# q for two tiles at a time behind k of the second one, G of both behind the next k

## The chip, the cores and the metric

The kernel runs on one core of one Trainium2 chip. The metric is device time in microseconds (us) of one execution, median of three runs. The core has five engines that work side by side, each in the order of its own program: TensorE (PE, with its weight loads as PEld), VectorE (DVE), ScalarE (ACT), GpSimd (POOL) and SyncE (SP), which here only issues DMAs and waits.

## The reference

Two blocks read x (2048 tokens of 640 numbers, bf16) and are added to it. The first is linear attention with 32 heads of 20 on the normalized xn, the second sends the 8 tokens with the largest router value through a gated MLP.

```python
xn = _layernorm(x)
# attention
q, k, v = split(xn @ wqkv)                    # 32 heads of 20
phi = lambda t: where(t > 0, t + 1, exp(t)) + 1e-6
pq, pk = phi(q), phi(k)
kv = einsum("bhsd,bhse->bhde", pk, v)
z = einsum("bhsd->bhd", pk)
num = einsum("bhqd,bhde->bhqe", pq, kv)
den = einsum("bhqd,bhd->bhq", pq, z)[..., None] + 1e-6
A = (num / den) @ wo
# eight tokens through the MLP
r = xn @ w_r
idx = argsort(-r)[:, :8]
y = (silu(xn[idx] @ w_gate) * (xn[idx] @ w_up)) @ w_down * sigmoid(r[idx])
B = xn + scatter(y, idx)
out = x + A + B
```

## The kernel before

The tokens are cut into 16 tiles of 128. v is never formed: instead of kv = pk' (xn wv) the kernel sums G = xn' pk over the tiles and multiplies by wv once. phi is written as min(exp(t), 1) + relu(t), so ACT makes two passes over the psum of k or q (Exp, Relu) and VectorE one that joins them.

The program is written out by hand: each engine executes its instructions in the order in which the source names them, and so do the DMA queues of SP, ACT and POOL. An instruction that waits holds up all behind it on its engine.

For each tile t there are these steps, by their names in the code:

- `ln_stats` (two `ln_half`, L163, and `ln_aggr`, L167) has VectorE take mean and variance of x; from tile 4 on POOL makes the reciprocal deviation out of it in four small steps (L171, L176, L178, L179).
- `ln_norm` (L191, VectorE) writes xn; from tile 3 on the same function issues a DMA transpose on SP (L196) that writes the tile's columns of xnT. Tiles 0 to 2 are transposed by TensorE (`tr_tile`) and copied out by `tr_evict`.
- `k_mm` (L236) makes k and, in a 641st column, the router value: five steps over D with 512 and 129 columns each, into the psum pair A. `k_phi` has ACT make both passes and copy the router value to r_all; `phi_vec` (L225, VectorE) writes pk.
- `q_mm` (L248) makes q transposed: 25 matmuls with wq as weights and 128 columns of xnT moving, into the psum pair B, then the two passes of ACT and one of VectorE (`q_phi`, L225) into pqT.
- `ga_mm` (L259) adds the tile's part of three fifths of G, three matmuls of 512 columns, with xn as weights and pk moving; its sums stay in the psum pair C and the bank D0 through the loop.

The loop over t issues, on TensorE, k(t), G(t-1), q(t). In the same round VectorE takes statistics of tile t + 3 and the norm of tile t + 2 (one more of each in round `CATCH` = 5, after which both are a tile further ahead), q of tile t - 1, and k of tile t. In the last rounds it also adds xn to x (`residual`, L360), and SP copies these sums to DRAM four tiles at a time (`keep`, L363).

`late_loads(t)` stands at the end of a round and issues the remaining loads on SP (L343), after the transposes that the round's norms issued: x of tiles 8 to 11 in round 2, x of tiles 12 to 15 in round 5, then wg and wu in rounds 6 to 11, wv and wo in 12 to 15, wd after the loop. `small_consts(t)` gives POOL a few small constants in rounds 3 to 6 and VectorE three small steps in round 12.

Behind the loop: four transposes of the router values (`pr`), G of the last tile, sums of pk over the tokens (`zp`, whose four parts go through small DMAs on SP and ACT, L477), the other two fifths of G (`gb1` 32 matmuls of 512 columns, L489, and `gb2` 80 of 128, L590), among them the search for the eight tokens on VectorE, the denominators (`pden`, L571, which reads all of pqT) and the MLP's products (`gu`, for which POOL gathers eight columns of xnT, L537). Then kv, M = kv wo, and the output tile by tile (L743, L751), 16 x 10 matmuls.

Of the kernel before, what the change touches and what calls it, by code (L numbers as in the profile page):

```python
# [8 lines left out]
P = 128  # L9
# [22 lines left out]
CATCH = 5  # L32
# [12 lines left out]
def kernel(  # L45
# [173 lines left out]
    def phi_vec(dst, er, as3):  # L219
        e, r = er  # L220
        ea, ra = e[:], r[:]
        if as3:
            ea = ea.rearrange("p (k f) -> p k f", k=KC)
            ra = ra.rearrange("p (k f) -> p k f", k=KC)
        nc.vector.scalar_tensor_tensor(  # L225
            out=dst, in0=ea, scalar=1.0, in1=ra, op0=ALU.min, op1=ALU.add
        )
# [16 lines left out]
    def q_mm(t, tag="B"):  # L244
        ps = pair(tag, f"q{t}")
        for m in range(KC):
            for kc in range(KC):
                nc.tensor.matmul(  # L248
                    ps[:, m * P : (m + 1) * P],
                    lhsT=wq[:, kc, m::KC],  # L250
                    rhs=xnT[:, kc, t * P : (t + 1) * P],
                    start=(kc == 0 and m in (0, 4)), stop=(kc == KC - 1),
                    skip_group_check=True,
                )
        return ps

# [84 lines left out]
    def late_loads(t):  # L341
        def part(dst, src, a, b):
# [7 lines left out]
            12: (wv, wv_v, 0, 2), 13: (wv, wv_v, 2, KC), 14: (wo, wo_v, 0, 4), 15: (wo, wo_v, 4, 8),  # L350
            16: (wd, kcD, 0, 6), 17: (wd, kcD, 6, 12),
# [14 lines left out]
    qer = None  # L366

    def q_phi(t, er):
        phi_vec(pqT[:, :, t * P : (t + 1) * P], er, True)

    def k_phi(t, kp):
        ker = phi_act(kp, "k")
# [3 lines left out]

    kp = k_mm(0, "A")
    tr1a, tr1b = bank("D1", "tr1a").bitcast(BF16), pair("C", "tr1b").bitcast(BF16)
# [4 lines left out]
    ln_stats(3)  # L383
    ker = k_phi(0, kp)
    kp = k_mm(1, "B")
    qp = q_mm(0, "A")
    ln_norm(2)
    phi_vec(pk[:, 0, :], ker, False)
    tr2 = bank("D1", "tr2").bitcast(BF16)
    tr_tile(2, tr2, 0, KC)  # L390
    ker = k_phi(1, kp)
    eq0 = phi_act(qp, "q", lambda: tr_evict(2, tr2, 0, KC, nc.scalar.copy))
    ln_norm(3)
    ln_stats(4)
    ga_mm(0)
    phi_vec(pk[:, 1, :], ker, False)
    qp = q_mm(1, "B")
    q_phi(0, eq0)
    qer = phi_act(qp, "q")

    for t in range(2, T):
        kp = k_mm(t)
        ga_mm(t - 1)
        qp = q_mm(t)
        for u in (t + 3, t + 4) if t == CATCH else (t + 3 + (t > CATCH),):
            if u < T:
                ln_stats(u)
# [399 lines left out]
```

## Time and profile before

| | us |
|---|---|
| median of three runs (111.18 to 112.16) | 111.19 |
| the profiled execution | 111.62 |
| its span, first to last instruction | 109.9 |
| TensorE busy | 105.5 |
| VectorE busy | 86.1 |
| ScalarE busy | 55.1 |
| GpSimd busy | 37.9 |

The median is what the change is compared by. All durations that follow come from the one profiled execution; it is 0.43 us above the median, and 1.7 us of it lie outside the span. A row of the chain shows start, duration, engine, tile name, line and count; a row of a group shows line, engine, operation, output and inputs, form and count, then busy time, the mean duration in ns, and the idle time of the engine just before, with what ended it. The mean duration of a matmul counts its whole way through the array; what a matmul costs in a stream is the time from one start to the next.

### The profile page before, as it was taken

How to read it: one execution, taken by the hardware profiler on the slowest of the kernel's cores; microseconds unless marked ns; L12 is line 12 of the kernel's file. 1: busy time of each engine (PE TensorE's matmuls, PEld its weight loads, DVE VectorE, ACT ScalarE, POOL GpSimd, SP SyncE). 2: the span in 40 equal slices, each digit the busy share in tenths (PEclk: the TensorE clock that was granted, in tenths of full speed). 3: DMA queues.
4: the chain of work that ended last, by engine and by line, in shares of the span. 5: the costliest groups of instructions: out<-in, count | busy, mean ns of one | idle time of the engine just before them, and what ended most of it. 6: DMA issues, size and time to landing. Idle time of an engine off the chain costs nothing.

```text
span 109.9 us, 2999 instructions
## 1 busy us (share of the span) xinstructions
PE 105.5 (96%) x1183; PEld 69.3 (63%) x1183; DVE 86.1 (78%) x205; ACT 55.1 (50%) x102; POOL 37.9 (34%) x83
## 2 busy tenths in 40 slices
PE   6998999999999999999999999999999999999990
PEld 2456866777577766777667744447995555555560
DVE  6889999887999889875999896951348967698680
ACT  4037987778867797777977745068028000000000
POOL 5414195989889955770000000240008100000000
DMA  2998164930569999998859970899541289997333
GB/s 72 335 375 292 33 36 75 283 66 3 118 177 321 220 267 280 316 305 224 290 187 285 292 257 5 232 378 372 175 145 51 15 228 323 340 387 277 128 119 119
DMA packets 25358, 23.09 MB, mean 210 GB/s; under 512 B 10624, under 2 KB 24064, under 8 KB 25344
## 3 DMA queue, kind: packets, MB, share of 16 engines
q1 hardware_dynamic: 22784, 20.43, 66.5%
q10 hardware_dynamic: 2384, 2.43, 6.4%
q8 instruction: 9, 0.15, 0.6%
q0 software_dynamic: 176, 0.04, 0.6%
q14 instruction: 5, 0.04, 0.1%
HBM read 14.94 MB, written 5.81 MB: 189 GB/s over the span
## 4 chain that ended last, share of the span: by engine, by line
PE 76%; DVE 10%; POOL 8%; issue 3%; DVEq 0%; POOLq 0%
PE o L743 14%; PE k L236 13%; PE q L248 13%; PE gbA L489 6%; PE gaC L259 5%; PE warm L271 4%; PE gbC L590 4%; POOL sq L176 3%; DVE st L163 2%; PE gaD L259 2%; DVE pk L225 2%; PE M L728 2%; POOL sc L178 2%; DVE xn L191 2%; PE gu L606 2%
## 5 line engine op out<-in xcount | busy, mean ns | idle before, releaser
L248 PEld LDWEIGHTS <-wq 128*128 128x128 bf16 x400 | 24.2, 117 | 3.4
L236 PE MATMUL k<-wk,xnT 128*128 128x512 bf16 (+1 forms) x160 | 24.8, 301 | 0.3 <-ACT xnT L206 0.3
L248 PE MATMUL q<-xnT,wq 128*128 128x128 bf16 x400 | 24.9, 220 | 0.0
L743 PEld LDWEIGHTS <-pqT 128*128 128x128 bf16 x165 | 12.8, 98 | 9.3
L236 PEld LDWEIGHTS <-xnT 128*128 128x128 bf16 x160 | 12.3, 98 | 8.5 <-ACT xnT L206 0.9
L213 ACT ACTIVATE eq<-q 128x640 bf16<-128x640 f32 x16 | 11.2, 703 | 10.5 <-PE q L248 10.5
L225 DVE SCALAR_TENSOR_TENSOR pk<-ek,rk 128x640 bf16<-128x640 bf16 x16 | 13.2, 824 | 3.6 <-ACT rk L216 3.4
L743 PE MATMUL o<-M,pqT 128*128 128x512 bf16 x110 | 15.8, 300 | 0.0
L176 POOL TENSOR_TENSOR sq<-sq,half 128x1 bf16<-128x1 bf16 x16 | 12.5, 778 | 6.2 <-DVE sc L175 4.0
L163 DVE BATCH_NORM_STATS2 st<-x_sb 128x6 f32<-128x320 bf16 x32 | 14.1, 480 | 0.4 <-DMA x_sb<-in_A_x_dram 0.4
L225 DVE SCALAR_TENSOR_TENSOR pqT<-eq,rq 128x640 bf16<-128x640 bf16 x16 | 13.2, 823 | 0.7 <-ACT rq L216 0.7
L213 ACT ACTIVATE ek<-k 128x640 bf16<-128x640 f32 x16 | 11.3, 705 | 1.6 <-PE k L236 0.4
L751 DVE TENSOR_TENSOR o_t<-o,x_sb 128x640 bf16<-128x640 f32 x11 | 8.8, 820 | 3.3 <-DMA x_sb<-xcp 1.7
L216 ACT ACTIVATE rq<-q 128x640 bf16<-128x640 f32 x16 | 11.2, 700 | 0.0
L216 ACT ACTIVATE rk<-k 128x640 bf16<-128x640 f32 x16 | 11.2, 699 | 0.0
L259 PE MATMUL gaC<-pk,xn 128*128 128x512 bf16 x32 | 9.5, 378 | 0.2 <-DVE pk L225 0.2
L537 POOL COPY xsT<-xnT 128x5 bf16 x8 | 1.9, 312 | 21.7 <-DVE icol L551 21.7
L178 POOL TENSOR_TENSOR sc<-sq,neg 128x1 f32<-128x1 bf16 x12 | 8.6, 716 | 0.9
L191 DVE TENSOR_SCALAR xn<-x_sb,sc 128x640 bf16<-128x640 bf16 (+2 forms) x17 | 6.9, 412 | 1.2 <-POOL sc L179 1.0
L489 PE MATMUL gbA<-pk,xn 128*128 128x512 bf16 x32 | 7.3, 380 | 0.0
L360 DVE TENSOR_TENSOR x_sb<-x_sb,xn 128x640 bf16<-128x640 bf16 x16 | 7.0, 482 | 0.0
L259 PEld LDWEIGHTS <-xn 128*128 128x128 bf16 x48 | 4.0, 97 | 4.1 <-issue 0.4
(152 smaller groups left out, 120.4 us busy)
## 6 DMA issues: line engine op xcount, KB each, us to landing
xcp<-x_sb SPq DMA_DIRECT2D x4, 640.0 KB, 5.2
x_sb<-in_A_x_dram SPq DMA_DIRECT2D x3, 640.0 KB, 4.7
wd<-in_B_w_down_dram SPq DMA_DIRECT2D x2, 960.0 KB, 6.6
x_sb<-xcp SPq DMA_DIRECT2D x3, 640.0 KB, 6.8
wg<-in_B_w_gate_dram SPq DMA_DIRECT2D x2, 768.0 KB, 6.6
wu<-in_B_w_up_dram SPq DMA_DIRECT2D x2, 768.0 KB, 5.3
out_dram<-o_t ACTq DMA_DIRECT2D x8, 160.0 KB, 2.7
out_dram<-o_t SPq DMA_DIRECT2D x7, 160.0 KB, 3.4
```

Source lines behind the costliest of these rows:

```text
L163: nc.vector.bn_stats(out=stat[t][:, h, :], in_=x_sb[:, t, h * HW : (h + 1) * HW])
L176: nc.gpsimd.tensor_tensor(out=sq[:, 1:2], in0=sq[:, 0:1], in1=half[:], op=ALU.pow)
L178: nc.gpsimd.tensor_tensor(out=sc[:, 1:2], in0=sq[:, 1:2], in1=neg1[:], op=ALU.pow)
L191: nc.vector.tensor_scalar(out=xn[:, t, a:b], in0=x_sb[:, t, a:b], scalar1=sc[:, 0:1], scalar2=sc[:, 1:2], op0=ALU.subtract, op1=ALU.mult,)
L213: nc.scalar.activation(e[:], ps[:, 0:D], AF.Exp)
L216: nc.scalar.activation(r[:], ps[:, 0:D], AF.Relu)
L225: nc.vector.scalar_tensor_tensor(out=dst, in0=ea, scalar=1.0, in1=ra, op0=ALU.min, op1=ALU.add)
L236: nc.tensor.matmul(ps[:, a:b], lhsT=xnT[:, kc, t * P : (t + 1) * P], rhs=wk[:, kc, a:b], start=(kc == 0), stop=(kc == KC - 1),)
L248: nc.tensor.matmul(ps[:, m * P : (m + 1) * P], lhsT=wq[:, kc, m::KC], rhs=xnT[:, kc, t * P : (t + 1) * P], start=(kc == 0 and m in (0, 4)) ...
L259: nc.tensor.matmul(gaC[:, c * TBLK : (c + 1) * TBLK] if c < 2 else gaD[:], lhsT=xn[:, t, c * P : (c + 1) * P], rhs=pk[:, t, 0:TBLK], start ...
L489: nc.tensor.matmul(gbA[:, (c - 3) * TBLK : (c - 2) * TBLK], lhsT=xn[:, t, c * P : (c + 1) * P], rhs=pk[:, t, 0:TBLK], start=(t == 0), stop ...
L743: nc.tensor.matmul(ps, lhsT=pqT[:, m, t * P : (t + 1) * P], rhs=M[:, m, a:b], start=(m == 0), stop=(m == KC - 1),)
```

## The change

The loop becomes one over pairs of tiles (t, t + 1), t even. TensorE issues in each round: k(t+1), four fifths of q for both tiles (`q2_mm` with `LO`, 20 matmuls of 256 columns, pair B), k(t+2), the last fifth of q (`HI`, five matmuls, bank D1), G(t), G(t+1). ACT makes its passes over 1024 and 256 columns in place of 640, VectorE likewise (`q2_vec`), and joins q of pair t - 2 in the round of pair t. `CATCH` is 4: in rounds up to 4 statistics are four tiles past t at the head of the round and five at its end, from round 6 on five and six. Round 4 has the additional tile of statistics and norm. `small_consts` and `late_loads` of both tiles stand at the end of the round, and in the plan wd now comes before wv and wo. Ten of the residuals are added in rounds 10 to 14, two more among the steps of the token search, and the copies to DRAM follow them. The transposes of the router values stand between q of the last pair and its G. Behind the loop `pc` is issued after three tiles of `gb1` in place of four, the two tiles of `gb2` ahead of `gu` are placed behind it, `ph` follows eleven tiles in place of twelve, and q of the last pair is joined after the search.

```diff
 LN_FAST = 4
 WARM = 10
 LAST = (0, 320, 512, 640)
-CATCH = 5
+CATCH = 4
 
 BF16 = mybir.dt.bfloat16
 F32 = mybir.dt.float32
...
             )
         return ps
 
-    def q_mm(t, tag="B"):
-        ps = pair(tag, f"q{t}")
-        for m in range(KC):
+    def q2_mm(t, ps, ms):
+        for n, m in enumerate(ms):
             for kc in range(KC):
                 nc.tensor.matmul(
-                    ps[:, m * P : (m + 1) * P],
+                    ps[:, n * 2 * P : (n + 1) * 2 * P],
                     lhsT=wq[:, kc, m::KC],
-                    rhs=xnT[:, kc, t * P : (t + 1) * P],
-                    start=(kc == 0 and m in (0, 4)), stop=(kc == KC - 1),
+                    rhs=xnT[:, kc, t * P : (t + 2) * P],
+                    start=(kc == 0 and n % 2 == 0), stop=(kc == KC - 1),
                     skip_group_check=True,
                 )
         return ps
+
+    def q2_tile(tag):
+        return work.tile([P, KC, 2 * P], BF16, tag=tag, name=tag)
+
+    def q2_act(dst, func, ps, ms):
+        n = len(ms) * 2 * P
+        nc.scalar.activation(
+            dst[:, ms[0] : ms[-1] + 1, :].rearrange("p m f -> p (m f)"), ps[:, 0:n], func
+        )
+
+    def q2_vec(t, er, ms):
+        a, b = ms[0], ms[-1] + 1
+        nc.vector.scalar_tensor_tensor(
+            out=pqT[:, a:b, t * P : (t + 2) * P], in0=er[0][:, a:b, :], scalar=1.0,
+            in1=er[1][:, a:b, :], op0=ALU.min, op1=ALU.add,
+        )
+
+    LO, HI = (0, 1, 2, 3), (4,)
 
     def ga_mm(t):
         for c in range(3):
...
             2: (x_sb, x_v, 8, 12), 5: (x_sb, x_v, 12, 16),
             6: (wg, kcF, 0, 2), 7: (wg, kcF, 2, 4), 8: (wg, kcF, 4, 5),
             9: (wu, kcU, 0, 2), 10: (wu, kcU, 2, 4), 11: (wu, kcU, 4, 5),
-            12: (wv, wv_v, 0, 2), 13: (wv, wv_v, 2, KC), 14: (wo, wo_v, 0, 4), 15: (wo, wo_v, 4, 8),
-            16: (wd, kcD, 0, 6), 17: (wd, kcD, 6, 12),
+            12: (wd, kcD, 0, 6), 13: (wd, kcD, 6, 12), 14: (wv, wv_v, 0, 2), 15: (wv, wv_v, 2, KC),
+            16: (wo, wo_v, 0, 4), 17: (wo, wo_v, 4, 8),
         }
         if t in plan:
             part(*plan[t])
...
         nc.sync.dma_start(xcp_v[:, a:b, :], x_sb[:, a:b, :])
 
 
-    qer = None
-
-    def q_phi(t, er):
-        phi_vec(pqT[:, :, t * P : (t + 1) * P], er, True)
-
-    def k_phi(t, kp):
-        ker = phi_act(kp, "k")
+    def k_vec(t, er):
+        phi_vec(pk[:, t, :], er)
+
+    def k_phi(t, kp, between=None):
+        ker = phi_act(kp, "k", between)
         nc.scalar.copy(r_all[:, t : t + 1], kp[:, D : D + 1])
         return ker
 
-
+    ker = {}
     kp = k_mm(0, "A")
-    tr1a, tr1b = bank("D1", "tr1a").bitcast(BF16), pair("C", "tr1b").bitcast(BF16)
+    tr1a, tr1b = bank("D1", "tr1a").bitcast(BF16), pair("B", "tr1b").bitcast(BF16)
     tr_tile(1, tr1a, 0, 2)
     tr_evict(1, tr1a, 0, 2, nc.scalar.copy)
     tr_tile(1, tr1b, 2, KC)
     tr_evict(1, tr1b, 2, KC, nc.vector.tensor_copy)
-    ln_stats(3)
-    ker = k_phi(0, kp)
-    kp = k_mm(1, "B")
-    qp = q_mm(0, "A")
+    ln_half(3, 0)
     ln_norm(2)
-    phi_vec(pk[:, 0, :], ker, False)
-    tr2 = bank("D1", "tr2").bitcast(BF16)
+    ln_half(3, 1)
+    ln_aggr(3)
+    ker[0] = k_phi(0, kp)
+    kp = k_mm(1, "C")
+    tr2 = bank("D0", "tr2").bitcast(BF16)
     tr_tile(2, tr2, 0, KC)
-    ker = k_phi(1, kp)
-    eq0 = phi_act(qp, "q", lambda: tr_evict(2, tr2, 0, KC, nc.scalar.copy))
+    k_vec(0, ker[0])
     ln_norm(3)
-    ln_stats(4)
-    ga_mm(0)
-    phi_vec(pk[:, 1, :], ker, False)
-    qp = q_mm(1, "B")
-    q_phi(0, eq0)
-    qer = phi_act(qp, "q")
-
-    for t in range(2, T):
-        kp = k_mm(t)
-        ga_mm(t - 1)
-        qp = q_mm(t)
-        for u in (t + 3, t + 4) if t == CATCH else (t + 3 + (t > CATCH),):
-            if u < T:
-                ln_stats(u)
-        for u in (t + 2, t + 3) if t == CATCH else (t + 2 + (t > CATCH),):
-            if u < T:
-                ln_norm(u)
-        q_phi(t - 1, qer)
-        ker = k_phi(t, kp)
-        if t > 12:
-            residual(4 * (t - 13) + 3)
-        phi_vec(pk[:, t, :], ker, False)
-        qer = phi_act(qp, "q")
-        if 11 < t < T - 1:
-            for u in range(4 * (t - 12), 4 * (t - 12) + 3):
+    ker[1] = k_phi(1, kp, lambda: tr_evict(2, tr2, 0, KC, nc.scalar.copy))
+
+    eqp = None
+    for t in range(0, T, 2):
+        if t > 0:
+            kp = k_mm(t + 1)
+            k_vec(t, ker[t])
+            ahead = 4 + (t > CATCH)
+            if t + ahead < T:
+                ln_stats(t + ahead)
+            if t + ahead - 1 < T:
+                ln_norm(t + ahead - 1)
+            ker[t + 1] = k_phi(t + 1, kp)
+        lo = q2_mm(t, pair("B", f"qlo{t}"), LO)
+        if t > 0:
+            q2_vec(t - 2, eqp, LO)
+            q2_vec(t - 2, eqp, HI)
+        eqp = q2_tile("eq"), q2_tile("rq")
+        q2_act(eqp[0], AF.Exp, lo, LO)
+        if t == T - 2:
+            break
+        kp = k_mm(t + 2)
+        ker[t + 2] = k_phi(t + 2, kp)
+        q2_act(eqp[1], AF.Relu, lo, LO)
+        hi = q2_mm(t, bank("D1", f"qhi{t}"), HI)
+        q2_act(eqp[0], AF.Exp, hi, HI)
+        q2_act(eqp[1], AF.Relu, hi, HI)
+        if t == 0:
+            ln_stats(4)
+            k_vec(1, ker[1])
+            ln_stats(5)
+            ln_norm(4)
+        else:
+            if t == T - 4:
+                for u in range(2, 5):
+                    residual(u)
+            k_vec(t + 1, ker[t + 1])
+            if t == CATCH:
+                ln_stats(t + 5)
+            if t + ahead < T:
+                ln_norm(t + ahead)
+            if t == CATCH:
+                ln_stats(t + 6)
+                ln_norm(t + 5)
+            elif t + ahead + 1 < T:
+                ln_stats(t + ahead + 1)
+        if t == T - 6:
+            for u in range(2):
                 residual(u)
-        small_consts(t)
-        late_loads(t)
-        if t > 12:
-            keep(4 * (t - 13), 4 * (t - 12))
-
-
+        if t == T - 4:
+            for u in range(5, 8):
+                residual(u)
+            keep(0, 4)
+        ga_mm(t)
+        ga_mm(t + 1)
+        for u in (t, t + 1):
+            small_consts(u)
+            late_loads(u)
+
+
+    q2_act(eqp[1], AF.Relu, lo, LO)
+    for u in (8, 9):
+        residual(u)
+    keep(4, 8)
+    late_loads(T - 2)
+    late_loads(T - 1)
+    k_vec(T - 1, ker[T - 1])
     pr = bank("D1", "pr").bitcast(BF16)
...
+    ga_mm(T - 2)
+    ga_mm(T - 1)
+    hi = q2_mm(T - 2, bank("D1", "qhi"), HI)
+    q2_act(eqp[0], AF.Exp, hi, HI)
+    q2_act(eqp[1], AF.Relu, hi, HI)
...
     )
     spread(0, 1, cand[:, 0:1, :])
     spread(1, 2, split[:])
+    residual(10)
 
     zp = pair("A", "zp")
 
...
                 tile_position=(0, 32 * i),
             )
 
-    ga_mm(T - 1)
     for t in range(T):
         z_mm(t)
     GT = sb([P, KC, D], BF16, "GT", tag="wk")
...
                 start=(t == 0), stop=(t == T - 1),
             )
 
-    for t in range(4):
+    for t in range(3):
         gb1(t)
     pc = bank("D1", "pc")
     nc.tensor.matmul(
...
         pc[:, 32:64], lhsT=ones4[:], rhs=candm[:, 2].rearrange("p b c -> p (b c)"),
         start=False, stop=True,
     )
-    for t in range(4, T):
+    for t in range(3, T):
         gb1(t)
...
     nc.vector.tensor_reduce(out=idx8[:], in_=eq[:], op=ALU.add, axis=AX.X)
     idxi = sb([P, C], I32, "idxi")
     nc.vector.tensor_copy(idxi[:], idx8[:])
-    q_phi(T - 1, qer)
+    residual(11)
+    keep(8, 12)
+    q2_vec(T - 2, eqp, LO)
+    q2_vec(T - 2, eqp, HI)
     _, toks = nc.values_load_multi_w_load_instructions(
         idxi[0:1, :], engines=[ENG.Pool], min_val=0, max_val=S - 1,
         skip_runtime_bounds_check_because="positions found among the tokens",
...
                 start=(t == 0 and c in (0, 4)), stop=(t == T - 1),
                 skip_group_check=True,
             )
-
-    for t in range(2):
-        gb2(t)
 
 
     gu = pair("A", "gu")
...
             op=ALU.mult,
         )
 
-    for t in range(2, 12):
+    for t in range(11):
         gb2(t)
     ph = bank("D1", "ph").bitcast(BF16)
     for b in range(3):
...
         in0=ph[:, 0:FJ].rearrange("p (n c) -> p n c", c=32)[:, :, 0:C],
         in1=gtb[:].unsqueeze(1).to_broadcast([P, FC, C]), op=ALU.mult,
     )
-    for t in range(12, T):
+    for t in range(11, T):
         gb2(t)
     nc.scalar.copy(GT[:, :, TBLK:D], gbC[:, 0:D].rearrange("p (c f) -> p c f", c=KC))
 
```

14 lines of the change are left out of this document (5 added, 9 removed).

## The prediction, before the result was known

> **What bounds the kernel now.** I read the share of each engine first, then the stages, then the chain.
>
> ```profile
> PE 105.5 (96%) x1183; PEld 69.3 (63%) x1183; DVE 86.1 (78%) x205; ACT 55.1 (50%) x102; POOL 37.9 (34%) x83
> ...
> 14.00:28.00 14.00, 14.00 (x158) 10.12 (x155) 12.06 (x28) 10.75 (x21) 11.79 (x28) 1.00 0.43 87
> 28.00:48.00 20.00, 19.77 (x218) 14.13 (x216) 17.94 (x37) 15.65 (x30) 15.64 (x31) 1.00 1.03 255
> ```
>
> The columns of the stages are PE, weight loads, DVE, ACT and POOL. The last number is GB/s. TensorE is busy for all of 14 to 28 us and misses 0.23 us of 28 to 48 us: it is the bound, and VectorE is second, with 18 of 20 us. So only two things can move the time: fewer TensorE nanoseconds, or new gaps on TensorE. One tile of the loop in the chain:
>
> ```profile
> 33.02 0.43 PE gaC L259 x2
> 33.46 0.21 PE gaD L259
> 33.67 1.40 PE q L248 x25
> 35.07 1.38 PE k L236 x10
> ```
>
> That is 0.65 (G), 1.40 (q) and 1.38 (k): 3.43 us a tile, without a gap.
>
> **q for two tiles.** 50 matmuls with 128 columns become 25 with 256. One with 128 costs 1.40 / 25 = 56 ns, one with 512 costs 0.43 / 2 = 215 ns; between them a matmul costs 2.9 ns and 0.414 ns a column, so one with 256 costs 109 ns. A pair of tiles takes 25 x 109 = 2.73 us for 2.80: 0.07 us less, **0.55 us over eight pairs**. The ends: nothing saved, or 256 columns at the rate of the 512 (108 ns), 0.10 us a pair, 0.8 us in all. So q alone, at its best, stays under 1% of the time, which is also about what a measurement of this kernel can tell from no change.
>
> ```profile
> L248 PEld LDWEIGHTS <-wq 128*128 128x128 bf16 x400 | 24.2, 117 | 3.4
> L213 ACT ACTIVATE eq<-q 128x640 bf16<-128x640 f32 x16 | 11.2, 703 | 10.5 <-PE q L248 10.5
> L482 ACT CAST GT<-gaC 128x1024 bf16<-128x1024 f32 x1 | 1.0, 1012 | 0.6 <-ACT zpart L473 0.6
> ```
>
> The Trainium skill (TensorE: Matmul & The Clock Gate, Back-to-back issue gap) gives a stream of load and matmul about 81 ns at 128 columns and 131 at 512; by that, an estimate, q would lose some 13 us. This case's trace has 56 and 215 ns (above), so it does not agree; what is left of the rule is a rival.
>
> ACT trades four passes of 640 columns a pair for two of 1024 and two of 256. From 703 and 1012 ns the slope is 0.8 ns a column, so 256 take about 0.39: 2.80 us for 2.81, and ACT waited 10.5 us for q. Nothing. VectorE writes the same 1280 columns in two pieces; the chain below has 0.73 for 640, and at 1.04 ns a column 1024 and 256 take 1.14 and 0.33, **1.47 us a pair** (ends 1.46 and 1.65, two passes at their full 0.82). The psum banks that k of tile 1, the transposes and both parts of q now use are emptied over 0.2 us before the next writer. Costs of the passes that follow:
>
> ```profile
> 12.06 0.80 DVE st L163 x2
> ...
> 12.89 0.22 DVE mv L167
> ...
> 27.92 0.73 DVE pqT L225
> 28.65 0.75 DVE pk L225
> ...
> 30.34 0.39 DVE L191 TENSOR_SCALAR xn<-x_sb,sc 128x640 bf16<-128x640 bf16 x1
> ...
> L171 POOL TENSOR_SCALAR sq<-mv 128x1 bf16<-128x1 bf16 x12 | 3.8, 317 | 6.8 <-DVE mv L167 6.8
> L176 POOL TENSOR_TENSOR sq<-sq,half 128x1 bf16<-128x1 bf16 x16 | 12.5, 778 | 6.2 <-DVE sc L175 4.0 <-DVE sq L171 1.1
> L178 POOL TENSOR_TENSOR sc<-sq,neg 128x1 f32<-128x1 bf16 x12 | 8.6, 716 | 0.9
> L179 POOL CAST sc<-mv 128x1 f32<-128x1 bf16 x12 | 3.6, 298 | 0.0
> ```
>
> So on VectorE: statistics of a tile 1.04, its norm 0.40, k 0.74. A pair needs 2.08 + 0.80 + 1.48 + 1.47 = 5.8 us, inside a pair of TensorE (2.73 + 2 x 1.38 + 2 x 0.65 = 6.79). POOL's four steps are 2.11 us, with the gaps between them about 2.4 from a tile's statistics to its norm when POOL is free.
>
> **The load that moves.** SP issues in the order of the program. Now, and the landing times of the first x load, of the transpose before it, and of the second x load:
>
> ```profile
> 12.09 5.40 SPq L196 DMA_TRANSPOSE xnT<-xn  x2
> 17.54 0.58 SPq L343 DMA_DIRECT2D x_sb<-in_A_x_dram  x1
> ...
> x_sb<-in_A_x_dram SPq DMA_DIRECT2D x1, 640.0 KB, 4.5
> xnT<-xn SPq DMA_TRANSPOSE x1, 2.6
> ...
> x_sb<-in_A_x_dram SPq DMA_DIRECT2D x1, 640.0 KB, 4.7
> ...
> L196 SPq DMA_TRANSPOSE xnT<-xn x13: 1200/1207/2636, 12.1 to 49.5; - x13
> ```
>
> Today x of tiles 8 to 11 is issued at 17.54, behind the transposes of tiles 3 and 4, and lands at 22.0. With the change the load stands at the end of the pair (2, 3), behind the transposes of tiles 5 **and 6**, while the statistics of tile 8 stand at the head of the next pair. I lay the rows on both queues.
>
> ```profile
> 10.23 1.56 PE L248 MATMUL q<-xnT,wq 128*128 128x128 bf16 x25
> 11.63 0.44 PE L200 MATMUL tr<-ident,xn 128*128 128x128 bf16 x5
> 11.91 0.60 PE L259 MATMUL gaC<-pk,xn 128*128 128x512 bf16 x2
> ...
> 15.81 0.45 DVE xn L191
> ```
>
> TensorE: k of tile 1 ends at 10.23; the transposes of tile 2 take 0.28 (11.63 to 11.91), four fifths of q 2.19, k of tile 2 1.38, the last fifth 0.55, G twice 1.30: 15.93. Two more pairs bring G of tile 4 to an end at 28.88, when G of tile 5 is due. VectorE: the norm of tile 4 still waits for POOL, begins at 15.81 as in the row, and ends at 16.26. Then k2 17.00, statistics 6 18.04, norm 5 18.45, q of pair 0 19.92, k3 20.66, norm 6 21.06. SP spends 1.2 us on that transpose and issues the load at 22.3; with 4.5 us it lands at **26.8**. VectorE has done statistics 7 and, behind k of tile 4 (20.88) and ACT's two passes of 0.70, k4 from 22.4 to 23.1; statistics 8 then wait **3.7 us**, and behind them in the queue are norm 7, q of pair 2 and k5, for which G of tile 5 waits. They end at 27.84, 28.24, 29.71 and 30.45: TensorE stands **1.6 us**.
>
> Nor is that all, for VectorE now has no lead, and this pair has three tiles of statistics and norms: from k5 to k7 lie 3 x 1.44 + 1.47 + 1.48 = 7.27 us, and norm 9 waits for POOL besides (statistics 9 end at 31.49, POOL at 33.9, VectorE was ready at 32.93). Then k6 ends at 35.04, statistics 11 at 36.08, norm 10 at 36.48, q at 37.95, k7 at 38.69; G of tile 7 was due at 30.45 + 6.79 = 37.24: **1.45 us**. The load of tiles 12 to 15 stands behind the transpose of tile 9 (34.3 + 1.2 + 4.7 = 40.2): statistics 12 end at 41.24, k8 at 41.98, statistics 13 at 43.02, norm 12 waits for POOL until 43.64 and ends at 44.04, q at 45.51, k9 at 46.25 against a due time of 45.48: **0.8**. One pair later k11 is in time. Together **3.8 us**.
>
> ```profile
> 18.56 0.22 DVE mv L167
> ...
> 21.48 0.18 POOL sc L179
> ```
>
> Ends: with POOL never late only 1.6 + 0.5 = 2.1; with POOL at 2.9 us a tile, as it has tile 6 now (from 18.78 to 21.66), and the first load at 4.7 too, about 5.9. I take 3.8, since its steps are the mean rows.
>
> **Dues that move, at nothing.** k of odd tiles comes up to 1.4 us earlier.
>
> ```profile
> xnT<-xn SPq DMA_TRANSPOSE x1, 3.8
> ...
> DMA to landing us min/median/max: 2.6/3.9/5.7
> ...
> PE gaC L259 <- DVE pk L225: 0.2, 1, 0.2
> DVE st L163 <- DMA x_sb<-in_A_x_dram: 0.4, 1, 0.4
> ```
>
> Tile 3's transpose (the first row) is issued at 12.09 as now, lands at 15.9 and is due at 15.93; tile 4's lands at 16.3 + 2.6 = 18.9 and is due at 19.5. If that cover goes, k pays what the transpose is late. The third row is the 0.23 us that TensorE loses now, before G of tile 4: it sits where G no longer stands, so I count it as saved.
>
> **The tail.** Its TensorE work only changes places.
>
> ```profile
> 66.74 5.29 PE gbA L489 x24
> 72.03 1.19 PE pden L571 x20
> ...
> 70.66 1.94 POOL L537 COPY xsT<-xnT 128x5 bf16 x8 [21.66 <-DVE icol L551]
> ```
>
> The router's matmul (pc) now stands behind six of these G matmuls instead of eight, and the experts' first product directly behind pden: between the two are 26 x 0.22 + 1.19 = 6.9 us, for which the gather on POOL needs 5.9 (from 66.74, where pc ends, to 70.66 + 1.94). If that cover goes, up to 1 us is lost. The q of the last pair is written behind the indices, 1.9 us with one residual, before pden asks for it. The residuals that come earlier (ten inside the loop) fall where statistics have ended. The loads of wd and wv and two copies of x now stand on SP ahead of the four small transfers of the sums of k: a rival, below.
>
> **Sum.** The profiled execution is 111.62 us (span 109.9, and 1.7 around it): -0.55 for q, -0.23 for the gap, +3.8 for the stalls, +3.0 in all, 114.6. The median of the runs is 0.43 below the profiled one: 111.19 + 3.0 = **114.2 us**; with the ends of the stalls, 112.5 to 116.3.
>
> **Rivals.** *The load is in time (not slower).* G of tile 5 waits for nothing if k5 ends by 28.88, so the load must land by 28.88 - 3.65 = 25.2, that is within 2.9 us of its issue. Then only the savings stay: 110.4 us. For it speaks that the DMA engines are nearly idle there (87 GB/s); against it that they are so today too, and the load takes 4.5. 0.10.
>
> *The transposes are late as well.* They land in 2.6 to 5.7 us, the longest with loads beside them; 1.4 us more at k3 or k10, 115.6. Against it: the rows around 16 us, alone, have 2.6. 0.07.
>
> *The sums of k wait in the queue.*
>
> ```profile
> wd<-in_B_w_down_dram SPq DMA_DIRECT2D x2, 960.0 KB, 6.6
> ```
>
> From the end of pair 12, some 60 us, SP has 2.0 MB of wd (the row), 0.8 of wv (640 x 640 in bf16) and two copies of four tiles of x, 0.66 each as the load above, ahead of the small transfers: 4.1 MB, at the 255 GB/s of the stage quoted first 16 us, to 76, where pden is due at 72.03 + 3.0 = 75. Up to 1 us more, 115.2. Against it: those 255 GB/s had the transposes among them. 0.08.
>
> *The clock drops.*
>
> ```profile
> L271 PE MATMUL warm<-zero 128*128 128x512 bf16 x10 | 4.4, 632 | 1.0 <-DVE zero L117 1.0
> ```
>
> The first ten matmuls, of 512 columns, take 0.44 us each, twice the 0.215 of later ones, so TensorE begins at half speed after standing idle. Should the gap at tile 5 bring that back for some 4 us, 2 us are added: 116.2. The same page of the Trainium skill (Part 1: The HAM clock gate) puts this at an idle window of about 3.4 us; no gap inside the run of before is long enough to show it. My gap is 1.6, and it decides only from a load that lands 2 us later still. 0.04.
>
> *Weight loads bound q.* If the 24.2 us of 400 loads were the bound, half of them would give 12.1 us back: 102 us with the stalls. The 56 ns against 215 / 4 = 54 for pure streaming speak against it. 0.01.
>
> **Numbers.** The forecast has 0.70. The range takes in its ends and the late transposes, sums and clock that stay under them, and leaves out the load in time and the weight loads: 112.3 to 116.5. Faster by over 1% (below 110.1) 0.02: the weight loads, or the load in time with savings just over their upper end; within 1% 0.11, the rest of the load in time and a forecast under its lower end; slower 0.87, all else.
>
> **What would show it.** In the changed profile VectorE's statistics wait for the load of x some 3.7 us, and again about 0.5, where today the same row says 0.4; SP issues that load near 22.3, behind the fourth transpose; TensorE's G waits for pk about 3.8 us in three pieces between 28 and 47 us, with the largest first, and is gapless after; 25 q matmuls of 256 columns take 2.73 us a pair. I am wrong if SP has the load before 20 us, or if G waits less than 1 us in all.

## The result, and the profile after

The changed kernel takes 118.46 us in the median of six executions (115.77 to 120.45), the kernel before beside it 111.27 (111.18 to 112.16). The ratio is **1.0445, with a 95% interval of 1.0364 to 1.0526**; it leaves out the executions that lie over 1.5% above the fastest, four of the six here, which is why it is below the ratio of the two medians. Slower was forecast, by 3%; it is 4 to 5%, about 116 us by the ratio, and the single executions lie further apart than those of the kernel before.

The profiled execution took 120.12 us against 111.62. Its page, with the clock granted to TensorE in 40 slices:

```profile
span 118.4 us, 2574 instructions
...
PEclk9999999999999999999999999999999589999999
```

The program has 425 instructions fewer than the 2999 of before and ends 8.5 us later; in one place near the end TensorE's clock was at half. The view of waits names what it waited for (engine and line, what ended the wait; us in total, times, the longest):

```profile
DVE xn L191 <- POOL sc L179: 4.7, 7, 1.5
...
DVE st L163 <- DMA x_sb<-in_A_x_dram: 4.1, 2, 3.9
...
DVE pqT L681 <- DMA rb<-rscr: 3.6, 1, 3.6
PE gaC L271 <- DVE pk L220: 3.3, 3, 1.9
...
DVE zc L591 <- DMA zrel<-zpart: 2.5, 1, 2.5
...
PE o L792 <- DVE pqT L681: 1.9, 1, 1.9
...
PE pden L623 <- DVE zm L595: 1.8, 1, 1.8
```

There are two groups. The first two rows and the fourth are the loop: VectorE's statistics wait 3.9 us for a load of x, and G waits for pk three times. The others are the tail: zm waits for the sums of k (zrel), which small DMAs move from rows to partitions, and pqT for the reciprocal denominators (rb), which are stored and broadcast. TensorE stands 1.8 us at pden and 1.9 us at the first output for them.

The loop, in SyncE's timeline and in those of VectorE and TensorE (start, duration, instruction, in brackets the idle time before it):

```profile
12.56 10.24 SPq L196 DMA_TRANSPOSE xnT<-xn  x4
22.85 0.58 SPq L355 DMA_DIRECT2D x_sb<-in_A_x_dram  x1
```

```profile
27.20 0.89 DVE L163 BATCH_NORM_STATS2 st<-x_sb 128x6 f32<-128x320 bf16 x2 [3.90 <-DMA x_sb<-in_A_x_dram]
...
30.03 0.82 DVE L220 SCALAR_TENSOR_TENSOR pk<-ek,rk 128x640 bf16<-128x640 bf16 x1
```

```profile
30.90 0.59 PE L271 MATMUL gaC<-pk,xn 128*128 128x512 bf16 x2 [1.94 <-DVE pk L220]
...
35.56 1.56 PE L231 MATMUL k<-wk,xnT 128*128 128x512 bf16 x9 [0.29 <-DMA xnT<-xn]
...
38.51 0.59 PE L271 MATMUL gaC<-pk,xn 128*128 128x512 bf16 x2 [0.21 <-DVE pk L220]
...
46.60 0.59 PE L271 MATMUL gaC<-pk,xn 128*128 128x512 bf16 x2 [1.14 <-DVE pk L220]
```

SyncE issues the load of tiles 8 to 11 at 22.85, behind four transposes, of which the fourth waits for tile 6 to be normalised. The load lands 4.3 us later; the statistics of tile 8, which VectorE has in front of pk of tile 5, start at 27.20; pk comes at 30.03, and G of tile 5 has waited 1.94 us. With k's wait for a transpose and the two later ones of G the idle times in brackets come to 1.94 + 0.29 + 0.21 + 1.14 = 3.6 us. They begin where the profile models the end of the last matmul; by its starts G of tile 5 is 2.11 us behind a gapless stream (30.90 against 28.57 + 0.22), so the loop loses a little more than their sum.

The tail, in SyncE's timeline and in the chain that ended last (start, duration, what the end waited on):

```profile
58.28 2.12 SPq L355 DMA_DIRECT2D wd<-in_B_w_down_dram  x2
...
63.22 2.40 SPq L355 DMA_DIRECT2D wv<-in_A_wqkv_dram  x2
68.97 2.10 SPq L526 DMA_DIRECT2D zrel<-zpart  x3
```

```profile
70.47 6.14 DMA zrel<-zpart
...
80.09 6.13 DMA rscr<-rden
86.28 4.09 DMA rb<-rscr
90.40 1.50 DVE pqT L681
```

The sums of k, 2.5 KB a transfer, are issued behind wd, wv and copies of x and take 6 us to land. The DMA view of the kernel before, and then of the changed one (size of one, median us from issue to landing), shows the sums (zrel), the store of the denominators (rscr) and their broadcast (rb) all slower:

```profile
rscr<-rden SPq DMA_DIRECT2D x1, 512.0 KB, 5.1
rb<-rscr SPq DMA_DIRECT2D x2, 256.0 KB, 2.5
...
zrel<-zpart SPq DMA_DIRECT2D x3, 2.5 KB, 2.2
```

```profile
rscr<-rden SPq DMA_DIRECT2D x1, 512.0 KB, 6.1
rb<-rscr SPq DMA_DIRECT2D x2, 256.0 KB, 4.2
...
zrel<-zpart SPq DMA_DIRECT2D x3, 2.5 KB, 6.8
zrel<-zpart ACTq DMA_DIRECT2D x1, 2.5 KB, 6.7
```

From the store of the denominators at 80.09 to pqT's end at 91.9 it is 11.8 us. TensorE ran out of other work in both stretches. What follows the second gap stands in the windows of the profile, one us each (busy time with instructions for PE, PEld, DVE, ACT, POOL; then the granted clock, DMA share, GB/s):

```profile
92.00:93.00 1.00, 0.78 (x4) 0.57 (x6) 1.00 (x2) 0.00 (x0) 0.00 (x0) 0.57 0.58 152
93.00:94.00 1.00, 1.00 (x6) 0.46 (x4) 1.00 (x2) 0.00 (x0) 0.00 (x0) 0.50 0.99 237
94.00:95.00 1.00, 1.00 (x7) 0.45 (x5) 1.00 (x2) 0.00 (x0) 0.00 (x0) 0.50 0.81 266
95.00:96.00 1.00, 1.00 (x7) 0.51 (x6) 1.00 (x1) 0.00 (x0) 0.00 (x0) 0.73 1.00 319
```

After 1.9 us without a matmul the clock is at half, and these four rows lose 0.43 + 0.50 + 0.50 + 0.27 = 1.7 us of full speed.

**The account of this execution** goes by the starts of TensorE's stages. The sums of k (zp), in the timeline of the kernel before and of the changed one:

```profile
63.48 1.28 PE L460 MATMUL zp<-pk,ones_bf 128*32 128x512 bf16 x32
```

```profile
66.91 1.28 PE L510 MATMUL zp<-pk,ones_bf 128*32 128x512 bf16 x32
```

They start 3.43 us later, which is what the loop has cost net of its savings; from there to pden it is 1.85 us more, from pden to the first output 1.73, and from there to the end of the span 1.49: 8.5 us in all. That is one execution; the fastest of the six took 115.77 at a clock of 1.0 throughout, so waits in the tail and the clock differ from one to the next.

### The profile page after: what moved, and what is told of

Same layout as the page of the kernel before. It is cut to its first block, busy times and chain, and to the rows that moved or that the text cites. A ratio compares the mean times of both kernels' runs of the same rounds, so it can differ in the third digit from the quotient of the medians.

```text
span 118.4 us, 2574 instructions
## 1 busy us (share of the span) xinstructions
PE 106.0 (90%) x971; PEld 68.9 (58%) x983; DVE 86.2 (73%) x205; ACT 54.5 (46%) x102; POOL 36.6 (31%) x83
## 4 chain that ended last, share of the span: by engine, by line
PE 43%; DVE 19%; DMA 17%; POOL 13%; issue 3%; SPq 2%; ACT 1%; DVEq 0%; POOLq 0%
PE o L792 14%; PE k L231 7%; PE qlo L242 6%; DMA zrel<-zpart 5%; DMA rscr<-rden 5%; DVE st L163 5%; POOL sq L176 5%; PE warm L283 4%; DMA x_sb<-in_A_x_dram 4%; DMA rb<-rscr 3%; POOL sc L178 3%; PE gaC L271 3%; DVE xn L191 3%; DVE pqT L262 3%; POOL sq L171 2%
## 5 line engine op out<-in xcount | busy, mean ns | idle before, releaser
L231 PE MATMUL k<-wk,xnT 128*128 128x129 bf16 (+1 forms) x153 | 24.3, 298 | 1.0 <-ACT xnT L206 0.3
L242 PEld LDWEIGHTS <-wq 128*128 128x128 bf16 x200 | 21.2, 117 | 1.9
L792 PE MATMUL o<-M,pqT 128*128 128x512 bf16 (+1 forms) x108 | 17.0, 317 | 2.2 <-DVE pqT L681 1.9
L242 PE MATMUL qlo<-xnT,wq 128*128 128x256 bf16 x160 | 18.8, 273 | 0.0
L176 POOL TENSOR_TENSOR sq<-sq,half 128x1 bf16<-128x1 bf16 x16 | 11.5, 719 | 6.7 <-DVE sc L175 4.7
L262 DVE SCALAR_TENSOR_TENSOR pqT<-eq,rq 128x1024 bf16<-128x1024 bf16 (+1 forms) x16 | 12.5, 823 | 0.2 <-ACT rq L256 0.2
L256 ACT ACTIVATE eq<-qlo 128x1024 bf16<-128x1024 f32 x8 | 8.2, 1023 | 6.3 <-PE qlo L242 6.3
L171 POOL TENSOR_SCALAR sq<-mv 128x1 bf16<-128x1 bf16 x12 | 6.0, 502 | 10.6 <-DVE mv L167 10.6
L681 DVE TENSOR_TENSOR pqT<-pqT,rb 128x2560 bf16<-128x2560 bf16 x4 | 5.9, 1485 | 3.6 <-DMA rb<-rscr 3.6
L256 ACT ACTIVATE rq<-qlo 128x1024 bf16<-128x1024 f32 x8 | 8.4, 1052 | 0.0
```

Source lines behind the costliest of these rows:

```text
L176: nc.gpsimd.tensor_tensor(out=sq[:, 1:2], in0=sq[:, 0:1], in1=half[:], op=ALU.pow)
L231: nc.tensor.matmul(ps[:, a:b], lhsT=xnT[:, kc, t * P : (t + 1) * P], rhs=wk[:, kc, a:b], start=(kc == 0), stop=(kc == KC - 1),)
L242: nc.tensor.matmul(ps[:, n * 2 * P : (n + 1) * 2 * P], lhsT=wq[:, kc, m::KC], rhs=xnT[:, kc, t * P : (t + 2) * P], start=(kc == 0 and n % ...
L256: nc.scalar.activation(dst[:, ms[0] : ms[-1] + 1, :].rearrange("p m f -> p (m f)"), ps[:, 0:n], func)
L262: nc.vector.scalar_tensor_tensor(out=pqT[:, a:b, t * P : (t + 2) * P], in0=er[0][:, a:b, :], scalar=1.0, in1=er[1][:, a:b, :], op0=ALU.min ...
L792: nc.tensor.matmul(ps, lhsT=pqT[:, m, t * P : (t + 1) * P], rhs=M[:, m, a:b], start=(m == 0), stop=(m == KC - 1),)
```

## The experiments

The theory: (1) the place of the load of tiles 8 to 11 in SyncE's queue makes the loop's loss; (2) loads in front of the small transfers make the tail's; (3) gaps near 2 us halve the clock, which adds to both. Rivals: the new order of TensorE's work loses time by itself; the tail is late only because the loop was.

### The changed kernel again

No edit.

> The changed kernel once more, in more executions: its time spreads over 4.7 us where the kernel before spreads over 1. Theory: the stalls of the loop are the same in each (G waits for pk 3.1 to 3.4 us), and the spread is in the tail, where the output waits for the broadcast of the denominators (1.9 us in the first profile) and the granted clock is at half for about 3 us after that wait in some executions and not in others (1.6 us). Rival: the spread comes from the loop, with different waits for x there.

117.64 us (117.19 to 120.18), ratio 1.0508 (1.0448 to 1.0568). In its profile, of an execution of 117.36 us, G of tile 5 waited about as long as in the first, but now the clock halved there; pden didn't wait, and the wait at the outputs was only 0.4 us. TensorE's timeline and two of the windows:

```profile
31.48 0.59 PE L271 MATMUL gaC<-pk,xn 128*128 128x512 bf16 x2 [2.07 <-DVE pk L220]
```

```profile
32.00:33.00 1.00, 1.00 (x6) 0.44 (x5) 0.97 (x4) 0.00 (x0) 0.36 (x2) 0.64 0.00 0
33.00:34.00 1.00, 1.00 (x6) 0.45 (x5) 0.78 (x3) 0.00 (x0) 0.92 (x2) 0.50 0.01 2
```

The starts of TensorE's stages in the three timelines (us):

| | sums of k | pden | first output | end of span |
|---|---|---|---|---|
| kernel before | 63.48 | 71.96 | 84.93 | 109.9 |
| changed, first profile | 66.91 | 77.24 | 91.94 | 118.4 |
| changed, second profile | 68.70 | 77.17 | 90.34 | 115.5 |

In the second profile 5.2 of the 5.6 us are lost ahead of the sums of k, 0.4 of them before the loop (k of tile 0 starts at 7.09 in place of 6.65), and the tail costs 0.4; in the first the tail costs 5.1. So the loop's loss is in both, the tail's in one. The expectation is half right: the tail differs most from one profile to the other, but the clock can fall at either place. It doesn't order the times either: the two executions at a clock of 1.0 took 117.33 and 117.92 us, the two at 0.985 117.19 and 117.36. What fills the time of the former isn't shown, since none of them was profiled.

### The load of tiles 8 to 11 a round earlier

```
-            2: (x_sb, x_v, 8, 12), 5: (x_sb, x_v, 12, 16),
+            1: (x_sb, x_v, 8, 12), 5: (x_sb, x_v, 12, 16),
```

> The load of x for tiles 8 to 11 is issued one pair earlier, behind the transpose of tile 4, all else as in the changed kernel. Theory (the late load makes the loop's stalls): VectorE's wait for x goes from 4.1 us to under 0.5, G waits for pk less than 0.6 us in all, the sums of k are reached 3 us earlier, and the time falls by 3 us, to about 113 us. Rival (three tiles of statistics in one pair, and POOL behind them, make the stalls): G still waits for pk 2 us or more, and the time stays above 115 us.

114.30 us (113.66 to 115.28), ratio 1.0233 (1.0179 to 1.0287): 3.3 us less than the changed kernel on the same chip, the clock at 0.997 or above in every execution. That is the theory's direction, but not all of it: about 113 us, under 0.5 us of waiting for x and under 0.6 for pk were expected. The waits of this kernel:

```profile
DVE st L163 <- DMA x_sb<-in_A_x_dram: 1.1, 3, 0.6
...
PE gaC L271 <- DVE pk L220: 1.0, 1, 1.0
...
PE pden L623 <- DVE zm L595: 0.8, 1, 0.8
PE k L231 <- DMA xnT<-xn: 0.6, 1, 0.6
```

The wait at tile 5 is gone, and with it both halvings. What stays is the wait at tile 9, where a norm ahead of pk on VectorE waits 1.5 us for GpSimd, 0.6 us at k for a transpose, and 0.8 us at pden. The tail's waits shrink too (pden from 1.8 to 0.8, none for pqT at the outputs), although nothing there was edited, which speaks in part for the second rival; but the second profile of the changed kernel had none at pden and 0.4 at the outputs, so this run alone can't decide it.

### The same fault in the kernel before

```
-            2: (x_sb, x_v, 8, 12), 5: (x_sb, x_v, 12, 16),
+            4: (x_sb, x_v, 8, 12), 5: (x_sb, x_v, 12, 16),
```

> The kernel before, with nothing changed but the load of x for tiles 8 to 11: it stands at the end of round 4, behind the transpose of tile 6, as in the changed kernel. Theory (the place of the load alone makes the stall, whatever the order of q and G): VectorE waits 3 to 4 us for x, TensorE waits 3 us or more for k or G soon after, and the time rises by 3 us or more, to 114.5 or above. Rival (the old order has the slack to hide it): under 112.5 us.

117.63 us (117.30 to 118.04), ratio 1.0518 (1.0477 to 1.0560). Its waits:

```profile
DVE st L163 <- DMA x_sb<-in_A_x_dram: 4.4, 3, 3.7
PE gaC L259 <- DVE pk L225: 4.0, 1, 4.0
```

One number in the old kernel, with the old order of q, G and router, gives a loss as large as the change's: 4.0 us of waiting in one piece, longer than any single wait of the changed kernel, and a clock of 0.971 to 0.985 in all four executions. In the profiled one the clock was still at 0.50 four us after the gap, which is about 2.5 us more; the sums of k start at 69.99, 6.5 us late, and from there on the stages take as long as before. So the misplaced load suffices, and the tail is not late here. That the first rival adds nothing in the changed kernel is for the last versions below to show.

### The large weights last, alone and with the earlier load

```
-            12: (wd, kcD, 0, 6), 13: (wd, kcD, 6, 12), 14: (wv, wv_v, 0, 2), 15: (wv, wv_v, 2, KC),
-            16: (wo, wo_v, 0, 4), 17: (wo, wo_v, 4, 8),
+            12: (wv, wv_v, 0, 2), 13: (wv, wv_v, 2, KC), 14: (wo, wo_v, 0, 4), 15: (wo, wo_v, 4, 8),
+            16: (wd, kcD, 0, 6), 17: (wd, kcD, 6, 12),
```

> The loads of wd stand behind the small transfers of the sums of k again and those of wv and wo ahead of them, as in the kernel before; x stays late. Theory (the small transfers wait behind 4 MB in the queue): they land within 3 us of their issue in place of 6 to 7, pden waits under 0.3 us for zm, and the time falls by 1.5 to 2 us; the loop's stalls stay at 3.1 us or more. Rival (any loads at that place hold them up, since 3 MB are left): they still take over 5 us and nothing is gained.

> Both: x one pair earlier and wd last. Theory: neither the loop's stalls nor the wait at pden is left, the output does not wait either, since what comes after pden is as in the kernel before, and the time is that of the kernel before less the saving of q: 110.4 to 111.2 us. Rival (something else in the new order costs as well, the passes of two tiles or the later residuals): above 112 us.

Alone it is slower still, 119.72 us (118.70 to 120.25), ratio 1.0693 (1.0632 to 1.0755). Its DMA view (the same columns) shows the cost moved:

```profile
rscr<-rden SPq DMA_DIRECT2D x1, 512.0 KB, 7.9
...
zrel<-zpart SPq DMA_DIRECT2D x3, 2.5 KB, 3.6
```

The sums of k land in 3.6 us and pden doesn't wait, as theory 2 says, though it didn't in the second profile of the changed kernel either, where they took 4.7. But wd now stands in front of the denominators, whose store takes 7.9 us; the outputs wait 2.3 us, and the clock is 0.971 to 0.986 in the six executions.

With the earlier load as well it is 117.81 us (116.84 to 119.31), ratio 1.0499 (1.0442 to 1.0556), where 110.4 to 111.2 were expected: a miss. Its store takes 7.6 us and its outputs wait 2.05 us, with half clock behind them; and the loop isn't clean either, since ahead of pk of tile 9 a norm waits 1.5 us for GpSimd and statistics 1.2 us for the load of tiles 12 to 15:

```profile
44.92 0.59 PE L271 MATMUL gaC<-pk,xn 128*128 128x512 bf16 x2 [2.15 <-DVE pk L220]
```

So the expectation had two things wrong: what is taken from in front of one transfer stands in front of the next, and the load of tiles 8 to 11 wasn't all that made the loop wait.

### Idle TensorE filled with unread matmuls

```
+        if t in (4, 6, 8):
+            for _ in range({4: 16, 6: 4, 8: 8}[t]):
+                nc.tensor.matmul(hi[:, 2 * P : 4 * P], lhsT=zero[:], ...
...
+    for _ in range(8):
+        nc.tensor.matmul(fill[:, 0:TBLK], lhsT=zero[:], ...
```

> The changed kernel with matmuls that nobody reads in TensorE's gaps: 16, 4 and 8 of 256 columns ahead of the second G of rounds 4, 6 and 8, and 8 of 512 columns ahead of the output. Theory (the gaps of 1.9 to 2.1 us are what halves the granted clock): the clock is 1.000 in all executions, none takes over 118.5 us, and the median falls by 0.5 to 1 us although some of the added matmuls fill gaps that an execution does not have. Rival (the clock falls for another reason): it is still 0.985 or less in half of the executions.

The clock stayed at 0.999 or 1.000 in all six executions, while statistics of tile 8 still waited 3.9 us: no gap in the profiled one is over 1.73 us. Without the filling the clock was at 0.992 or below in 8 of 12 executions, so theory 3 is borne out. The time did not follow: 121.25 us (120.90 to 122.08), ratio 1.0866 (1.0828 to 1.0904), as the filling matmuls had a wait of their own:

```profile
PE qhi L459 <- ACT rq L256: 5.2, 3, 1.7
```

They write into a bank that ScalarE still reads. This waiting and the filling itself, an estimated 28 x 0.109 + 8 x 0.215 = 4.8 us of matmuls, are more than the clock and the waits that they replace were worth.

### The loads of x and GpSimd's constants moved, then every late load

In the first only the two loads of x move, a round earlier, and GpSimd's small constants wait until the loop's tight part is over; wd, wv and wo stay where the change put them. In the second every late load is issued one or two tiles earlier than in the changed kernel, x between the two tiles of a pair, and the constants wait as well. Neither is the old order: x of tiles 12 to 15 and wd come earlier than in the kernel before.

```
-            2: (x_sb, x_v, 8, 12), 5: (x_sb, x_v, 12, 16),
+            1: (x_sb, x_v, 8, 12), 3: (x_sb, x_v, 12, 16),
...
-            small_consts(u)
+            if u > 6:
+                small_consts(u)
             late_loads(u)
+        if t == 10:
+            for u in range(3, 7):
+                small_consts(u)
```

```
-            2: (x_sb, x_v, 8, 12), 5: (x_sb, x_v, 12, 16),
+            2: (x_sb, x_v, 8, 12), 4: (x_sb, x_v, 12, 16),
...
                 ln_norm(t + ahead - 1)
+            if t < T - 2:
+                late_loads(t)
...
-        for u in (t, t + 1):
-            small_consts(u)
-            late_loads(u)
+        if t >= 12:
+            small_consts(t)
+        late_loads(t + 1)
...
```

> The changed kernel with both loads of x one pair earlier and POOL's small constants behind its last statistics, the other loads as they are. Theory: against the kernel with only the first x earlier, the wait of G of tile 9 (1.0 us) goes, since neither x nor POOL is late for tiles 11 and 12: about 113 us, 1 us less. The wait at pden for the sums of k (0.8 us) stays. Rival (VectorE itself is too full for three tiles in one pair): G of tile 7 or 9 still waits 0.8 us or more.

> The changed kernel with every late load one or two tiles earlier (x of tiles 8 to 11 behind the transpose of tile 5, of tiles 12 to 15 behind that of tile 7, one load after the first norm of a pair and one at its end, so that wd, wv and wo are issued by the end of the loop) and POOL's small constants behind its last statistics. Theory: the loop waits under 0.6 us in all, the small transfers of the sums of k find an empty queue and land in 2 to 4 us, nothing of wd or wo is left beside the denominators, and the time is that of the kernel before less 0.5 to 0.8 us for q: 110.5 to 111.3. Rival (the transposes pay for the earlier loads): k waits for xnT 1 us or more, and the time stays above 112.

111.71 us (110.97 to 113.28), ratio 0.9985 (0.9955 to 1.0016), and 111.51 (110.92 to 115.79), ratio 0.9982 (0.9952 to 1.0012): level with the kernel before, and the first 1.3 us better than the 113 expected. TensorE's longest wait behind its first matmuls, in the first of the two:

```profile
PE k L231 <- DMA xnT<-xn: 0.8, 1, 0.8
```

G, pden and the outputs have no row there. So the whole loss was in where loads and constants were issued; q for two tiles, G of two together, statistics five ahead and the router in the pair cost nothing that the time shows, and bring no more than 0.5%, the end of both intervals. Three of the second version's twelve executions took 114.5 to 115.8 us, at a clock of 0.985; their cause is open.

The first version also answers the second rival. Its large loads stand in front of the sums of k as in the changed kernel, and still, by its DMA view,

```profile
zrel<-zpart SPq DMA_DIRECT2D x3, 2.5 KB, 2.9
```

What differs is the time between them. Seven of the traces have wd, wv and two copies of x in front of the sums, in the changed kernel's order. From the end of wv's issue to the issue of the sums they leave 3.4, 4.2, 4.6, 5.2, 6.0, 6.2 and 6.2 us, and the sums take 6.8, 5.5, 4.7, 3.9, 3.2, 2.9 and 3.0 us to land. So the loads do hold the sums, as theory 2 has it, as long as they were issued shortly before; with the loop in time, pden doesn't wait. Both theory and rival hold in part.

### Copies of x behind the denominators, and pden earlier

```
-    keep(8, 12)
...
-    keep(T - 4, T)
...
+    keep(8, 12)
+    keep(T - 4, T)
     for j in (0, 2):
```

```
-    for t in range(3, T):
+    for t in range(3, 14):
         gb1(t)
...
     nc.scalar.activation(rden[:], lden[:], AF.Exp, scale=-1.0)
+    for t in range(14, T):
+        gb1(t)
```

> The kernel with the loads spread, and the two copies of x to DRAM (tiles 8 to 15, 1.3 MB) issued behind the store of the denominators in place of ahead of it. Theory (what is left in the tail is the queue ahead of that store): the store lands in 4 us or less in place of 5.9, VectorE no longer waits for the broadcast (2.0 us), the executions over 114 us, in which the output waits and the clock falls, are gone, and the median is 110.8 to 111.3. Rival (the store and the broadcast take that long by themselves): they land as before and the median stays at 111.5.

> The same, and the denominators' product 0.9 us earlier: ahead of the last two tiles of G's fourth and fifth part. Theory: it waits for the sums of k, which land just then, so it gains no more than 0.3 us over the one before: 110.6 to 111.2. Rival: the chain from it to the output is what bounds, and the whole 0.9 us is gained.

> Both of these edits on the kernel with only x and POOL's constants earlier (wd, wv and wo as in the changed kernel). Theory (the loads of the loop need not be spread if the tail's queue is in the better order): within 0.4 us of the one before. Rival: wo, still issued after the sums of k, holds the store of the denominators, and it is 1 us slower.

The copies moved in the version with all loads spread: 112.53 us, ratio 1.0078 (1.0047 to 1.0108). pden earlier too: 113.04, 1.0128 (1.0085 to 1.0171). Both edits in the other version: 112.68, 1.0111 (1.0064 to 1.0158). All three are slower, by 1 to 1.5%, than the versions that they start from. With the copies moved (the first of the three) the outputs' sums on VectorE wait longer for x to come back from DRAM, 1.7 us at most where it was 0.9 in the kernel before, and TensorE waits 0.8 us for VectorE there:

```profile
DVE o_t L805 <- DMA x_sb<-xcp: 3.2, 3, 1.7
```

And in the last of the three, by its DMA view, the store is faster and the broadcast slower:

```profile
rscr<-rden SPq DMA_DIRECT2D x1, 512.0 KB, 3.3
rb<-rscr SPq DMA_DIRECT2D x2, 256.0 KB, 5.9
```

Together they take 9.2 us, where the version that it starts from has 8.6 (5.5 + 3.1). With only the copies moved it is 8.9 (5.1 + 3.8), against 9.7 (5.9 + 3.8) ahead of that; the 4 us or less that were expected of the store did not come there. Why the broadcast takes what the store gives back isn't settled by these runs.

### q in halves again

```
-                nc.tensor.matmul(
-                    ps[:, n * 2 * P : (n + 1) * 2 * P],
+                for h in range(2):
+                    nc.tensor.matmul(
+                        ps[:, (2 * n + h) * P : (2 * n + h + 1) * P],
...
```

> The kernel with x and POOL's constants earlier, and q made with 50 matmuls of 128 columns a pair again, in the same order and the same banks. Theory: 25 x (2 x 56 - 109) ns = 0.07 us a pair come back, 0.55 us in all, so the time is 0.3 to 0.8 us above the same kernel with 256 columns (111.71). Rival (weight loads bound q): 2 us or more; or the loop's other engines hide it all: no difference.

In the version with two loads of x moved, q of a pair as 50 matmuls of 128 tokens takes, by the chain of this kernel,

```profile
11.10 2.23 PE qlo L243 x40
...
14.71 0.56 PE qhi L243 x10
```

2.79 us, against 2.73 for 25 of 256, by the chain of the version that it starts from:

```profile
25.08 2.18 PE qlo L242 x20
...
28.64 0.55 PE qhi L242 x5
```

The time is 111.55 us (110.88 to 112.97), ratio 0.9973 (0.9949 to 0.9998), against 0.9985 with the long matmuls. The 0.3 to 0.8 us that were expected of taking the saving away do not show: a saving of half a microsecond on TensorE's own time was not seen in the whole, as far as two intervals of about 0.3% each way can tell.

## Why the prediction was right, and where it wasn't

**The load of x: right in place and size.** Forecast were an issue at 22.3, a landing at 26.8 and 3.7 us of waiting; it was 22.85, 27.2 and 3.9. G of tile 5 was to lose 1.6 us and waited 1.94, in the second profile 2.07. The run with the load earlier (3.3 us less) and the old kernel with nothing but its load later (ratio 1.0518) show it as the cause, and not only as a wait beside it.

**G of tile 7: mis-sized.** 1.45 us were expected, 0.21 came, and in the second profile no such wait is listed. One half is GpSimd's part of the norm of tile 9, taken at the mean of its rows, 2.4 us from the statistics, which is 1.8 here, so that VectorE waits 0.49 us where the prediction had 0.97:

```profile
33.73 0.44 DVE L191 TENSOR_SCALAR xn<-x_sb,sc 128x640 bf16<-128x640 bf16 x1 [0.49 <-POOL sc L179]
```

The other half is TensorE: from G of tile 5 to where G of tile 7 is due it takes 7.4 us, with k's late transpose in it, where the forecast had 6.79.

**G of tile 9: the size near, the cause another.** 0.8 us were expected, 1.14 came, 1.53 in the second profile. The prediction laid it to the load of tiles 12 to 15. In the first profile the norm of tile 11, ahead of pk of tile 9, waits 1.53 us for GpSimd, which first makes the small constants of the round (35.4 to 37.8 in its timeline), a step that the prediction had left out for this round; the load is no more than 0.2 us late behind it. With the first load earlier the two are 1.5 and 0.6. In the version that moves constants and load G has no such wait; which of the two moves would do alone wasn't tried. That the loop's waits, 3.6 us, come near the forecast's 3.8 is luck in part, since one stall was overpriced and the others were longer.

**q and the old gap: right as durations.** 2.73 us a pair, and no wait where the 0.23 had been. That the 0.55 would reach the end is not borne out: the run with q in halves was no slower.

**The transposes were in time** at k of tile 3, as costed; at k of tile 8 one was 0.29 late.

**"Its TensorE work only changes places": the step that did not hold.** The tail was priced at nothing; it cost 5.1 us in the first profile and 0.4 in the second. The rival with the sums of k in the queue, given 0.08 and up to 1 us, happened in the first, with 1.8 us, and its own sum was close: it had the loads done at 76 us with pden due at 75, and the trace has the sums landed at 76.6 with TensorE ready for pden at 75.45. It left out two steps of VectorE between landing and pden, 0.6 us, and its low chance was the mistake. The store and the broadcast of the denominators were not in the prediction at all; they take 10.3 us in the first profile and 9.6 in the second where they took 7.6, and TensorE waited 1.88 and 0.35 us for them.

**The clock: a rival that came, with the wrong threshold.** It had 0.04 and was to decide only from a load 2 us later still, a gap of some 3.6 us. The rows show half clock after 1.88 us (the outputs, first profile) and 2.07 us (G of tile 5, second), and none after the 1.94 and 1.79 us that the first profile also has. The Trainium skill (TensorE: Matmul & The Clock Gate, Part 1: The HAM clock gate) gives an idle window of about 3.4 us ahead of the slow clock, and says that this window runs freely. The trace doesn't agree with 3.4 us as a limit for a gap, since 1.88 us were enough; that the same gap decides in one execution and not in the next would fit a window that runs freely, but no run here shows the window.

So the sum had the loop alone: 3.0 us more were forecast, and up to the sums of k it was 3.43 in the first profile and 5.2 in the second, there with half clock. Tail and clock, two rivals that were set apart as if only one thing could happen, came on top, since each is set off by the waits that the forecast itself had. The range to 116.5 held the ratio's 116 us, but partly by luck: its upper end stood for longer stalls, and what filled it were clock and tail. By the second series (ratio 1.0508, 116.8 us) it would have been just outside.

## What to carry to other kernels

When the order of a loop is changed, write down anew for every load what stands in front of it in its queue, what that waits for, and who reads the load first: here one load behind one waiting transpose was worth 3.3 us, and the same fault alone made the old kernel 5% slower. The same goes for small work on a side engine: GpSimd's constants held a norm for 1.5 us. Moving a load away from one small transfer puts it in front of another, so the whole order of the queue is priced, not a pair. A gap of about 2 us on TensorE can be followed by half clock that costs up to 1.7 us, and needs a line in the sum, not only a rival; here executions with and without it took the same 117.2 to 117.9 us.

## What was not expected of the hardware

- The clock halves after gaps of about 2 us in some executions and not in others of the same kernel. In the profiled executions it fell after gaps of 1.88 (changed kernel, first profile), 2.05 (x earlier and wd last), 2.07 (changed kernel, second), 2.33 (wd last alone) and 4.00 us (the old kernel with its load late), and did not after 2.15 (x earlier and wd last), 2.01 (wd last alone), 1.94 and 1.79 (changed kernel, first) or the three of 1.73 (the filled kernel). After the first four it cost 1.70 or 1.71 us each by the windows, which is 3.4 us at half speed. What decides between 1.88 and 2.15 us stays open, and so do the gaps of the executions without a profile.
- A transfer of 2.5 KB (the sums of k) lands in 2.2 us in the kernel before and in 6.8 when large loads were issued 3.4 us ahead of it. From ScalarE's queue it takes 6.7, much the same, so the order of SyncE's own queue is not all of it.
